# First MLP's single slots: Square, Tanh, h*e, h − tanh(h) and the copies of y at a higher scheduling priority

## The chip, the cores and the metric

The kernel runs on one core of a Trainium2 chip. The metric is the device time of one execution in microseconds (us). The engines that matter are TensorE (PE, matmuls; PEld is its weight load), VectorE (DVE), ScalarE (ACT), GpSimd (POOL) and SyncE (SP), which issues the DMAs. Each engine takes its instructions in the order in which they were laid down; one that waits for a semaphore holds up all that stand behind it on that engine.

## The reference

Four batches b, 8 heads, 576 tokens, 64 numbers per head; x is 2304 × 512 and both MLPs go 512 → 2048 → 512:

```
A  = softmax(q @ k_lm.T / 8)      # k_lm, q_lm: means of k, q over 18 tokens each, 32 landmarks
Bm = softmax(q_lm @ k_lm.T / 8);  C = softmax(q_lm @ k.T / 8)
Z  = Newton iteration for inverse(Bm), 6 times:  Z = 2 Z - Z Bm Z
x  = concat_heads(A @ Z @ C @ v)
h  = x @ w1_in;  x = (h - tanh(h)) @ w1_out                       # first MLP
h  = x @ w2_in;  out = (h * tanh(log(1 + exp(h)))) @ w2_out       # second MLP
```

## The kernel before, in words

The attention's last product is fused with the first MLP. P = (Z·C·v)·w1_in is formed for a pair of heads, A is transposed to AT, and h = P·AT comes out directly. P, AT, weights and the activations g are split into a high and a low part; three matmuls (hi·hi, lo·hi, hi·lo) replace one of full precision. From slot 16 on g is split as well.

**Slots.** The first MLP is cut into 128 slots. Slot s has batch b = s // 32, half batch hf = s // 16 % 2 (288 tokens) and feature block f = s % 16, so its h is a 128 × 288 tile. Slots below 24 and from 104 on (`WIDE = (24, 104)`) go in pairs through one PSUM tile `hw` of two banks (`vec`). Slots 24 to 103 go one by one (`vec_one`) through two single PSUM banks `h`, used in turn. The change touches `vec_one` and `y1`.

**One single slot s**, in the order of the program text:
- ACT splits the high part of gg of slot s − 2 (L115), and POOL or DVE its low part (L116).
- PE has written h(s) (L773, or L777 to L779 where AT is split). ACT takes Square into e (L852) and Tanh into t (L853).
- POOL makes the mask e ≥ FT (mk, L854). ACT takes Exp and Square of e into q (L856, L857).
- DVE does for slot s − 1: g = q·g (`small`, L800), then the pick where the mask is set (`pick`, L804).
- DVE does for slot s: g = h·e (L865) and t = h − tanh(h) (L867). L867 is the last reader of h(s): when it ends, the bank is free for h(s + 2).
- PE does y1 of an older slot (LAG = 4): y += w·gg (L882, L883, L886). Four PSUM banks y hold a half batch's four 128 × 288 sums over its 16 slots. At f = 15 four ACT copies (L891, two for each half of the feature blocks) take y to SBUF, an SP DMA writes it to DRAM (ys, L892), and the next half batch's y1 may then start in these banks.

**What sets the order.** A tile scheduler places the instructions of a slot with those of the background: the next batch's attention (landmark means L424 on DVE, L433 and L435 on ACT; the Newton products L377 with L614 on DVE; the transposes and normalisation of A and C L666 to L696; P in L736 and L738), the first MLP's weights (L303, L305), and from slot 102 on the second MLP's weights and y in (L914 and others). It orders by a priority that `tc.high_priority(n)` raises by n places; `yield` in a slot's generator lets another stream's instruction come next in program order. From slot 116 on (SWITCH) the order is that of the program text.

The tiles' names in the rows: es = e, qs = q, ta = t, tb and tc = g of two pairs of slots in turn, mk = mask, raw = the copy of y in SBUF, c = a row block of A or C, yv = Newton's Z.

Of the kernel before, what the change touches and what calls it, by code (L numbers as in the profile page):

```python
# [15 lines left out]
ACTF = mybir.ActivationFunctionType  # L16
ALU = mybir.AluOpType
# [12 lines left out]
def kernel(  # L30
# [68 lines left out]
    V = nc.vector  # L99
    A = nc.scalar  # L100
# [39 lines left out]
    def raw_f32():  # L140
        return f32(raw_p.tile([128, 512, 4], U16, tag="raw", name="raw").rearrange("p f t -> p (f t)"))
# [601 lines left out]
    hp, sv, yps = {}, {}, {}  # L743
# [42 lines left out]
    def low_half(s):  # L786
        gg = gg_tile(s, F32R)
        with tc.high_priority(20):
            split(sv[s], gg[:, 0], gg[:, 1], late())
        sv[s], sv[s + 1] = gg[:, :, 0], gg[:, :, 1]  # L790

    def low_one(s):
        gg = (ggs[s - 1] if s % 2 else gg_tile(s, F32R))[:, :, s % 2]
        with tc.high_priority(20):
            split(sv[s][0], gg[:, 0], gg[:, 1], late())
        sv[s] = gg

    def small(g, q):
        with tc.high_priority(40):
            V.tensor_tensor(out=g, in0=q, in1=g, op=ALU.mult)  # L800

    def pick(g, mk, t):
        with tc.high_priority(40):
            V.copy_predicated(out=g, mask=mk, data=t)  # L804
# [39 lines left out]
    def vec_one(s):  # L844
        i = s % 2
        if s == WIDE[0]:
            low_half(s - 2)
        elif s > WIDE[0] + 1:
            low_one(s - 2)
        h, e, q, mk = hp.pop(s), ES[:, i], QS[:, i], MK[-1][:, i]  # L850
        t, g = TA[:, i], (TB, TC)[s // 2 % 2][:, i]
        A.activation(out=e, in_=h, func=ACTF.Square)  # L852
        A.activation(out=t, in_=h, func=ACTF.Tanh)  # L853
        G.tensor_scalar(out=mk, in0=e, scalar1=FT, scalar2=None, op0=ALU.is_ge)  # L854
        with tc.high_priority(40):
            A.activation(out=q, in_=e, func=ACTF.Exp, scale=FK)  # L856
            A.activation(out=q, in_=q, func=ACTF.Square, scale=FB, bias=bias_c[:, 0:1])  # L857
        sv[s] = (g, t, q, mk)
        if s > WIDE[0]:
            g0, t0, q0, mk0 = sv[s - 1]  # L860
            small(g0, q0)
            yield 0
            pick(g0, mk0, t0)
            yield 0
        V.tensor_tensor(out=g, in0=h, in1=e, op=ALU.mult)  # L865
        yield 0
        V.tensor_tensor(out=t, in0=h, in1=t, op=ALU.subtract)  # L867
        yield 1

    def y1(s, half):  # L870
        f = s % 16
        gg = sv[s]
        w = W1o[f]
        for d in (2 * half, 2 * half + 1) if s < NW else ():
            if f == 0:
                yps[d] = ps_y.tile([128, 512], F32, tag="y", name="y")[:, 0:HS]
            mm(yps[d], w[:, 0, 128 * d:128 * d + 128], gg, start=(f == 0), stop=(f == NF - 1))
        for d in (2 * half, 2 * half + 1) if s >= NW else ():
            if f == 0:
                yps[d] = ps_y.tile([128, 512], F32, tag="y", name="y")[:, 0:HS]  # L880
            c = slice(128 * d, 128 * d + 128)
            mm(yps[d], w[:, 0, c], gg[:, 0, :], start=(f == 0), stop=False)  # L882
            mm(yps[d], w[:, 1, c], gg[:, 0, :], start=False, stop=False)  # L883
        for d in (2 * half, 2 * half + 1) if s >= NW else ():
            c = slice(128 * d, 128 * d + 128)
            mm(yps[d], w[:, 0, c], gg[:, 1, :], start=False, stop=(f == NF - 1))  # L886
        if f == NF - 1:
            o = (raw_f32() if s < NS - 1 else p2["yf"].tile([128, 2, C2], F32, tag="yf", name="yf").rearrange(
                "p a n -> p (a n)"))[:, 0:2 * HS].rearrange("p (d n) -> p d n", d=2)
            for d in range(2):  # L890
                A.activation(out=o[:, d], in_=yps[2 * half + d], func=ACTF.Copy)  # L891
            nc.sync.dma_start(out=ys[s // 16][:, 2 * half:2 * half + 2], in_=o)  # L892


# [162 lines left out]
    def pair(s, bg):  # L1057
        cur[0] = s
        v = vec(s) if wide(s) else None
        if s == WIDE[1]:  # L1060
            two_banks()
        if v:
            h1(s)
            h1(s + 1)
        for i in (s, s + 1):
            cur[0] = i
            if not v:
                h1(i)
            if i >= LAG:
                y1(i - LAG, 0)  # L1070
            mix, tail = bg(i)
            for g in mix + tail:
                part(g)
            if i >= LAG:
                y1(i - LAG, 1)
            parts([v or vec_one(i)] + mix)
            parts(tail)
# [4 lines left out]
    def group(k, bg2):  # L1082
        if k:
            units = o2_units(k - 1)
        for p in range(7):
            product(k, p)
            if k:
                for _ in range(UNITS[p]):
                    next(units)
            else:  # L1090
                for x in LAST[p]:
                    y1(NS - LAG + x // 2, x % 2)
                if p == 5:
                    ph1.close()
                    for name, bufs in (("g3", 3), ("yl", 2), ("st", 2)):
                        p2[name] = ctx.enter_context(tc.tile_pool(name=name, bufs=bufs))
            mix = bg2(k, p)
            for g in mix:
                part(g)
            parts([combine(k, p)] + mix)  # L1100
        if k:
            assert next(units, None) is None
# [240 lines left out]
```

## Time and profile before

| | |
|---|---|
| median of 3 runs | 824.63 us (822.94, 824.63, 828.34) |
| the profiled execution | 824.84 us; its span on the core 823.1 us |
| PE busy | 786.2 us, 96% of the span |
| DVE, ACT, POOL busy | 587.2, 494.9, 192.9 us (71%, 60%, 23%) |
| first MLP's single slots | about 116 to 364 us of the span |
| second MLP | about 446 us to the end |

The span is what the core's instructions cover; the execution's own time is 1.7 us longer. The page gives busy time by engine, the span in 40 slices, the chain of work that ended last, groups of instructions by line, and DMA issues. In the rows further down, "[0.75 <-DVE ta L867]" says that the engine sat idle for 0.75 us before this row and that the write of ta by DVE at line 867 released it. Consecutive rows of an engine overlap a little, since instructions are pipelined: the cost of one is better read from start to start.

### The profile page before, as it was taken

What the parts mean: (1) busy time and instruction counts of PE and PEld (TensorE: products, weight loads), DVE (VectorE), ACT (ScalarE), POOL (GpSimd) and SP (SyncE); (2) the same over time, 40 slices, a digit from 0 to 9 for tenths busy, and PEclk for the clock granted to TensorE, in tenths of its full rate; (3) what the DMA queues carried; (4) which work ended last, traced back from release to release, by engine and by line L of the source; (5) the groups of instructions that cost most, each with busy time, mean ns of one, the idle gap of its engine ahead of it and who ended that gap; (6) DMA issues with size and microseconds to landing.
All of it is one profiled execution on the core that took longest, in us unless ns stands there. A gap on an engine that the chain in (4) does not pass through costs nothing. (4 is left out here: it accounts for less than half of the span.)

```text
span 823.1 us, 14641 instructions
## 1 busy us (share of the span) xinstructions
PE 786.2 (96%) x5473; PEld 677.4 (82%) x5473; DVE 587.2 (71%) x1179; ACT 494.9 (60%) x1102; POOL 192.9 (23%) x215
## 2 busy tenths in 40 slices
PE   8889999999999999989998999999999999999996
PEld 4556787799978888779997888888888888889885
DVE  7799999898699977899987877885333356334332
ACT  5677877787678876785786566556223236223222
POOL 0000028765678656752220000000000000000000
PEclk9999999999999999999999999999999999999999
DMA  8898933414043001150327757864425424523402
GB/s 275 268 310 290 362 111 101 155 37 146 1 160 133 1 31 53 52 157 1 131 90 251 247 209 274 279 231 163 179 90 186 160 91 152 193 90 114 155 1 76
DMA packets 42022, 123.61 MB, mean 150 GB/s; under 512 B 5856, under 2 KB 14560, under 8 KB 38880
## 3 DMA queue, kind: packets, MB, share of 16 engines
q1 hardware_dynamic: 41952, 122.68, 42.5%
q8 instruction: 43, 0.70, 0.4%
q14 instruction: 27, 0.22, 0.1%
HBM read 94.36 MB, written 28.31 MB: 149 GB/s over the span
## 5 line engine op out<-in xcount | busy, mean ns | idle before, releaser
L983 ACT ACTIVATE gg<-x 128x384 fp32r<-128x384 f32 x72 | 37.8, 525 | 170.4 <-DVE x L993 170.4
L882 PE MATMUL y<-gg,w 128*128 128x288 f32 x448 | 132.8, 311 | 5.0 <-ACT raw L891 3.9
L883 PE MATMUL y<-gg,w 128*128 128x288 f32 x448 | 125.9, 295 | 0.0
L854 POOL TENSOR_SCALAR mk<-es 128x288 uint8<-128x288 f32 x80 | 78.5, 982 | 138.2 <-DVE yv L614 114.4
L882 PEld LDWEIGHTS y<-gg,w 128*128 128x128 f32 x448 | 84.1, 188 | 24.4 <-issue 15.2
L972 PE MATMUL h<-yk,P 128*128 128x384 f32 x288 | 97.6, 339 | 3.4 <-DVE P L208 3.4
L970 PE MATMUL h<-yk,P 128*128 128x384 f32 x288 | 97.5, 338 | 1.7 <-ACT yf L891 0.6
L971 PE MATMUL h<-yk,P 128*128 128x384 f32 x288 | 96.9, 336 | 0.0
L886 PE MATMUL y<-gg,w 128*128 128x288 f32 x448 | 96.0, 295 | 0.0
L986 DVE TENSOR_TENSOR gg<-x,gg 128x384 fp32r<-128x384 f32 x72 | 40.2, 558 | 68.4 <-ACT x L984 66.6
L883 PEld LDWEIGHTS y<-gg,w 128*128 128x128 f32 x448 | 84.3, 188 | 0.7 <-issue 0.2
L993 DVE TENSOR_TENSOR x<-x,h 128x384 f32<-128x384 f32 x72 | 39.8, 552 | 57.9 <-PE h L972 57.9
L1030 PE MATMUL y<-w,gg 128*128 128x512 f32 x192 | 76.3, 398 | 0.0
L1029 PE MATMUL y<-w,gg 128*128 128x512 f32 x192 | 76.2, 397 | 0.0
L1028 PE MATMUL y<-w,gg 128*128 128x512 f32 x192 | 75.8, 395 | 0.0
L886 PEld LDWEIGHTS y<-gg,w 128*128 128x128 f32 x448 | 71.8, 188 | 0.2
L970 PEld LDWEIGHTS h<-yk,P 128*128 128x128 f32 x288 | 54.3, 189 | 9.7 <-issue 1.4
L151 ACT ACTIVATE top<-raw 128x512 f16<-128x512 bf16 x64 | 49.9, 786 | 20.2 <-DVE X L185 6.1
L972 PEld LDWEIGHTS h<-yk,P 128*128 128x128 f32 x288 | 54.3, 189 | 5.9 <-DVE P L208 5.9
L971 PEld LDWEIGHTS h<-yk,P 128*128 128x128 f32 x288 | 54.2, 188 | 5.9
L116 POOL TENSOR_TENSOR gg<-tc,gg 128x288 fp32r<-128x288 f32 (+1 forms) x45 | 39.9, 894 | 39.6 <-ACT gg L115 36.0
L116 POOL TENSOR_TENSOR gg<-tb,gg 128x288 fp32r<-128x288 f32 (+1 forms) x44 | 40.4, 922 | 32.3 <-ACT gg L115 24.5
(214 smaller groups left out, 1947.2 us busy)
## 6 DMA issues: line engine op xcount, KB each, us to landing
P<-w2s SPq DMA_DIRECT2D x16, 1024.0 KB, 4.8
w<-w1s SPq DMA_DIRECT2D x24, 512.0 KB, 4.4
P<-w2s SPq DMA_DIRECT2D x16, 768.0 KB, 5.7
w2s<-P SPq DMA_DIRECT2D x8, 1024.0 KB, 3.9
raw<-in_w1i_dram SPq DMA_DIRECT2D x16, 511.8 KB, 5.1
raw<-in_w1o_dram SPq DMA_DIRECT2D x16, 511.8 KB, 5.1
raw<-in_w2i_dram SPq DMA_DIRECT2D x16, 511.8 KB, 4.2
raw<-in_w2o_dram SPq DMA_DIRECT2D x16, 511.8 KB, 4.5
```

The source lines that it names most:

```text
L116: eng.tensor_tensor(out=L, in0=src, in1=f32(H), op=ALU.subtract)
L151: A.activation(out=top[:, :, 1], in_=raw.bitcast(BF16)[:, :, 2], func=ACTF.Copy)
L854: G.tensor_scalar(out=mk, in0=e, scalar1=FT, scalar2=None, op0=ALU.is_ge)
L882: mm(yps[d], w[:, 0, c], gg[:, 0, :], start=(f == 0), stop=False)
L883: mm(yps[d], w[:, 1, c], gg[:, 0, :], start=False, stop=False)
L886: mm(yps[d], w[:, 0, c], gg[:, 1, :], start=False, stop=(f == NF - 1))
L970: mm(t, w[:, i, 0, c], y[a][:, 0], start=(a == 0), stop=False)
L971: mm(t, w[:, i, 0, c], y[a][:, 1], start=False, stop=False)
L972: mm(t, w[:, i, 1, c], y[a][:, 0], start=False, stop=(a == 1))
L1028: mm(q, gg[:, 0, cs], w[:, 0, :], start=first, stop=False)
L1029: mm(q, gg[:, 0, cs], w[:, 1, :], start=False, stop=False)
L1030: mm(q, gg[:, 1, cs], w[:, 0, :], start=False, stop=last)
```

## The change

Square and Tanh of a single slot, h·e and h − tanh(h), and the two copies per half of a y go into blocks `tc.high_priority(70)`; the `yield 0` between h·e and h − tanh(h) goes. No instruction is added or removed: each engine has the same ones in another order. `small`, `pick`, Exp and Square of e keep their 40, the splits their 20.

```diff
         t, g = TA[:, i], (TB, TC)[s // 2 % 2][:, i]
-        A.activation(out=e, in_=h, func=ACTF.Square)
-        A.activation(out=t, in_=h, func=ACTF.Tanh)
+        with tc.high_priority(70):
+            A.activation(out=e, in_=h, func=ACTF.Square)
+            A.activation(out=t, in_=h, func=ACTF.Tanh)
         G.tensor_scalar(out=mk, in0=e, scalar1=FT, scalar2=None, op0=ALU.is_ge)
...
-        V.tensor_tensor(out=g, in0=h, in1=e, op=ALU.mult)
-        yield 0
-        V.tensor_tensor(out=t, in0=h, in1=t, op=ALU.subtract)
+        with tc.high_priority(70):
+            V.tensor_tensor(out=g, in0=h, in1=e, op=ALU.mult)
+            V.tensor_tensor(out=t, in0=h, in1=t, op=ALU.subtract)
         yield 1
...
-            for d in range(2):
-                A.activation(out=o[:, d], in_=yps[2 * half + d], func=ACTF.Copy)
+            with tc.high_priority(70):
+                for d in range(2):
+                    A.activation(out=o[:, d], in_=yps[2 * half + d], func=ACTF.Copy)
             nc.sync.dma_start(out=ys[s // 16][:, 2 * half:2 * half + 2], in_=o)
```

The lines of the kernel after are one to two numbers higher: L852, 853, 856, 857, 865, 867, 891, 892 become L853, 854, 857, 858, 867, 868, 893, 894.

**Place A: ACT while the wide slots 18 and 19 run** (99 to 103 us), where the first half batch's last y copy falls. L817, L818, L828 and L829 are the wide form of a slot's Square, Tanh, Exp and Square; L115 splits gg of slots 16 and 17; L303 is weights. Before, and then after:

```order
L817 ACTIVATE es<-hw 128x576
L818 ACTIVATE tb<-hw 128x576
L828 ACTIVATE qs<-es 128x576
L115 ACTIVATE gg<-tc 128x576
L829 ACTIVATE qs<-qs,bias_c 128x576
L303 ACTIVATE w<-w 128x512
L891 ACTIVATE raw<-y 128x288
```

```order
L817 ACTIVATE es<-hw 128x576
L893 ACTIVATE raw<-y 128x288
L828 ACTIVATE qs<-es 128x576
L818 ACTIVATE tb<-hw 128x576
L829 ACTIVATE qs<-qs,bias_c 128x576
L115 ACTIVATE gg<-tc 128x576
L303 ACTIVATE w<-w 128x512
```

The copy went up five places, and the split of gg now stands behind the copy and behind the second exponential step. On SP the DMA of this copy (L892, now L894) now stands before both of the next batch's loads of k (L408); it stood between them.

**Place B: DVE in slots 29 to 31** (133 to 137 us). L682 and L684 belong to the normalisation of C, L696 transposes it, L738 is the low part of P, L424 a landmark mean of k. Before, and then after:

```order
L738 TENSOR_TENSOR P<-m,P 128x512
L684 RECIPROCAL xm<-xm 128x9
L424 TENSOR_REDUCE red<-k 128x64
L865 TENSOR_TENSOR tb<-h,es 128x288
L867 TENSOR_TENSOR ta<-h,ta 128x288
L800 TENSOR_TENSOR tb<-qs,tb 128x288
L696 STREAM_TRANSPOSE c<-c 128x288
```

```order
L696 STREAM_TRANSPOSE c<-c 128x288
L684 RECIPROCAL xm<-xm 128x9
L738 TENSOR_TENSOR P<-m,P 128x512
L867 TENSOR_TENSOR tb<-h,es 128x288
L868 TENSOR_TENSOR ta<-h,ta 128x288
L696 STREAM_TRANSPOSE c<-c 128x288
L800 TENSOR_TENSOR tb<-qs,tb 128x288
L424 TENSOR_REDUCE red<-k 128x64
```

The mean stood ahead of the pair that frees the bank of h and now stands behind it; one transpose came ahead of the pair in its place.

**Place C: ACT where half batch 1 is copied out** (slots 35 and 36, 151 to 156 us). L736 is the high part of P, L115 AT<-c the high part of AT. Before, and then after:

```order
L115 ACTIVATE gg<-tb 128x288
L852 ACTIVATE es<-h 128x288
L853 ACTIVATE ta<-h 128x288
L856 ACTIVATE qs<-es 128x288
L891 ACTIVATE raw<-y 128x288
L857 ACTIVATE qs<-qs,bias_c 128x288
L891 ACTIVATE raw<-y 128x288
L736 ACTIVATE P<-m 128x512 x2
L115 ACTIVATE AT<-c 128x288
L891 ACTIVATE raw<-y 128x288 x2
```

```order
L853 ACTIVATE es<-h 128x288
L854 ACTIVATE ta<-h 128x288
L857 ACTIVATE qs<-es 128x288
L893 ACTIVATE raw<-y 128x288 x2
L858 ACTIVATE qs<-qs,bias_c 128x288
L115 ACTIVATE gg<-tb 128x288
L736 ACTIVATE P<-m 128x512 x2
L115 ACTIVATE AT<-c 128x288
L893 ACTIVATE raw<-y 128x288 x2
```

Copies 1 and 2 came up beside each other, and the split of gg went down. Copies 3 and 4 still stand behind P and the AT split.

## Rows read from the trace of the kernel before

**Rows 1.** Windows by stage: length, busy us of each engine, clock, DMA share, GB/s.

```profile
core 0: us, PE busy (x) PEld busy (x) DVE busy (x) ACT busy (x) POOL busy (x), PEclk, DMA share, GB/s
24.00:130.00 106.00, 97.77 (x772) 69.88 (x765) 97.17 (x187) 81.54 (x162) 10.45 (x11) 1.00 0.73 255
130.00:227.00 97.00, 94.20 (x900) 82.36 (x898) 82.89 (x195) 74.56 (x209) 65.65 (x76) 1.00 0.28 93
```

**Rows 2.** PE's waits: line that waited, releaser, us in total, times, longest.

```profile
PE y L882 <- ACT raw L891: 3.9, 4, 1.8
...
PE h L777 <- DVE ta L867: 2.9, 4, 1.3
PE hw L777 <- DVE ta L867: 2.0, 1, 2.0
```

**Rows 3.** Timeline of PE, rows at which it waited: start, length, instruction, wait.

```profile
100.81 0.53 PE L377 MATMUL m<-yv 32*32 32x96 f32 x16 [0.55 <-DVE yv L614]
101.73 0.40 PE L882 MATMUL y<-gg,w 128*128 128x288 f32 x1 [0.39 <-ACT gg L115]
...
136.05 0.75 PE L773 MATMUL h<-AT,P 128*128 128x288 f32 x2 [0.75 <-DVE ta L867]
...
155.98 0.40 PE L882 MATMUL y<-gg,w 128*128 128x288 f32 x1 [1.56 <-ACT raw L891]
...
234.34 0.40 PE L777 MATMUL h<-AT,P 128*128 128x288 f32 x1 [1.25 <-DVE ta L867]
...
352.02 0.40 PE L882 MATMUL y<-gg,w 128*128 128x288 f32 x1 [1.76 <-ACT raw L891]
```

**Rows 4.** Timeline of DVE at places B and C.

```profile
133.98 1.29 DVE L424 TENSOR_REDUCE red<-k 128x64 f32<-128x1152 f32 x1
135.19 0.44 DVE L865 TENSOR_TENSOR tb<-h,es 128x288 f32<-128x288 f32 x1
...
152.75 0.44 DVE L680 TENSOR_REDUCE xm<-c 128x9 f32<-128x288 f32 x1
153.11 0.58 DVE L804 COPY_PREDICATED tc<-mk,ta 128x288 f32<-128x288 uint8 x1
...
154.32 0.45 DVE L800 TENSOR_TENSOR tc<-qs,tc 128x288 f32<-128x288 f32 x1
154.69 0.47 DVE L696 STREAM_TRANSPOSE c<-c 128x288 f32<-128x288 f32 x1
```

**Rows 5.** Timeline of ACT at place C.

```profile
153.44 1.10 ACT L736 ACTIVATE P<-m 128x512 fp32r<-128x512 f32 x2
155.19 0.44 ACT L115 ACTIVATE AT<-c 128x288 fp32r<-128x288 f32 x1 [0.64 <-DVE c L696]
155.54 0.69 ACT L891 ACTIVATE raw<-y 128x288 f32<-128x288 f32 x2
```

**Rows 6.** Timeline of ACT at place A.

```profile
99.34 0.65 ACT L817 ACTIVATE es<-hw 128x576 f32<-128x576 f32 x1
99.89 0.65 ACT L818 ACTIVATE tb<-hw 128x576 f32<-128x576 f32 x1
100.42 0.69 ACT L828 ACTIVATE qs<-es 128x576 f32<-128x576 f32 x1
101.00 0.68 ACT L115 ACTIVATE gg<-tc 128x576 fp32r<-128x576 f32 x1
101.57 0.78 ACT L829 ACTIVATE qs<-qs,bias_c 128x576 f32<-128x576 f32 x1
```

**Rows 7.** Timeline of SP's queue at place A: the load of k, the store of y.

```profile
98.86 0.39 SPq L408 DMA_DIRECT2D k<-in_kT_dram  x1
```

**Rows 8.** The source line L408, all its loads from issue to landing.

```profile
DMA to landing us min/median/max: 3.8/6.0/8.9
```

**Rows 9.** Source lines L867 and L800: shortest, median and longest ns, then the forms.

```profile
L867 DVE TENSOR_TENSOR ta<-h,ta x80: 438/446/451, 118.7 to 363.8; 128x288 f32<-128x288 f32 x80
...
L800 DVE TENSOR_TENSOR tb<-qs,tb x46: 416/460/1478, 47.6 to 419.5; 128x288 f32<-128x288 f32 x40, 128x576 f32<-128x576 f32 x6
```

## The prediction

> **What bounds the kernel now.** I read the windows by stage first [rows 1]. In 130 to 227 us PE is busy for 94.20 of 97 us at full granted clock, and over the whole span the page has it at 96%. So the kernel is bound by PE almost everywhere, and only PE's idle time can be won. DVE (82.89 of 97) is next. The early stage, 24 to 130 us, is different: PE 97.77 and DVE 97.17 of 106, so there DVE is nearly as full as PE, and what is put ahead of something on DVE or ACT can reach PE.
>
> Next I read PE's waits by releaser [rows 2]. The change can only shorten waits for the banks of h (released by L867) and of y (released by the copies L891). They are 3.9 us in four waits on copies, 2.9 + 2.0 us in five waits on L867, and one more of 0.75 us at 136.05 [rows 3]: 9.5 us together, 1.2% of the time. That is the ceiling. It is concentrated in few places, so I went through these one by one: what stands before the releaser on its engine, and whether the new order moves it. The timeline of PE has the places [rows 3].
>
> **The change part by part.** Nothing is added, so each term is a place where the order differs.
>
> *Place B, 136.05 us.* PE waits 0.75 us for L867. On DVE the mean L424 starts at 133.98 and the pair at 135.19 [rows 4]: the mean costs the pair 1.21 us. It now stands behind the pair, and one transpose L696 (some 0.4 us, its row at 154.69 lasts 0.47 [rows 4]) stands ahead instead. The pair gains 1.21 − 0.40 = 0.8 us, more than the wait. Term: −0.75 us (between 0, if the transpose waits for POOL, and −0.75).
>
> *Place C, 151 to 160 us.* PE waits 1.56 us at 155.98 for copies 3 and 4 [rows 3]. They stand behind the AT split, which itself waited 0.64 us for DVE's transpose L696 [rows 5]. The copies were raised, yet in the new order they are still behind that split. What changes is that on DVE the L696 now comes ahead of an L800 (154.32 to 154.69, 0.37) and of L680 (152.75 to 153.11, 0.36) [rows 4]: 0.73 us earlier. ACT itself is done with P by 153.44 + 1.10 = 154.54 [rows 5], so the split can start at most 0.65 us earlier; the copies follow it. A little later PE waits for L867: rows 2 leave 2.9 − 1.25 − 1.3 = 0.35 us for two small waits [rows 2, 3], of which I count one, 0.2, here; it goes if the mean of q that stands before it on DVE is not late. I take −0.7 us for the place (bounds 0, if POOL delays L696, and −1.76, both waits).
>
> *The same switch in slots 67 and 68.* Rows 2 leave 3.9 − 1.56 − 1.76 = 0.6 us for the two smaller waits on copies, and the other half of the 0.35 us for L867. I take −0.2 us (0 to −0.8).
>
> *234.34, 331 and 352.02 us.* The two long waits on L867 (1.25 us at 234.34 [rows 3], and the 1.3 us that is the longest of its row [rows 2]) and the 1.76 us for copies at 352.02 [rows 3] are half of the ceiling. There ACT, DVE and POOL order the instructions ahead of the releaser as before: at 234 and 331 an L738 of two products stands ahead of the pair still, and copies 3 and 4 at 352 are behind the AT split still. Term: 0 for 4.3 us of waits.
>
> *Slots 102 to 106.* PE waits 2.0 us for L867 at the first wide h after the single slots [rows 2]. An L804 (0.58 us at most, by the row at 153.11 [rows 4]) stood ahead of the pair there and now stands behind it, but PE also reaches the first wide h three y matmuls sooner (0.4 us), so nothing of its own is won there; the matmuls that it passes are still worth their time later. I take −0.4 us (0 to −0.8).
>
> *Place A, 99 to 105 us: a loss.* The split of gg (L115) starts at 101.00 and its first reader on PE at 101.73 [rows 3, 6]. With the copy and the second exponential step ahead, the order L817, copy, L828, L818, L829, L115 gives, start to start from the rows: 99.34 + 0.55 + 0.29 + 0.58 + 0.53 + 0.67 = 101.96 instead of 101.00: 0.96 us later [rows 6] (0.29 is my value for one copy: two together last 0.69 [rows 5]). PE fills 0.53 us of this with a third Newton product that the new order pulls ahead (one x16 lasts 0.53 [rows 3]), which leaves 0.4 us. On DVE the mean L424 moves from 116.8 us to just behind the mask of slots 20 and 21, ahead of the wide pair that frees hw; by its length of 1.29 us [rows 4] the pair and the low split come 1.2 us later, and against a PE that idles 8 us in this stage [rows 1] I take half of it as lost, 0.7 us. Together +1.1 us. The lower bound is 0 (both covered), the upper +4.1 (rival 2).
>
> Of the rest: Square and Tanh in the middle of a batch already stand first in a slot, and the position of h against y1 on PE is the same in slots 25 to 103, so I give it nothing; what covers it is that PE is 97% busy there.
>
> Sum: −0.75 − 0.7 − 0.2 − 0.4 + 1.1 = −0.95 us. After each of these places PE is the bound, so a shift carries through to the end. From the profiled execution's own 824.84 us: 823.9 us. The median of the runs lies 0.2 us below that execution, so **823.7 us**.
>
> **The rivals.**
>
> *1. All waits that it aims at vanish.* From 9.5 us, nothing lost early: 824.6 − 9.5 = 815.1, or some 816 if the smaller ones stay. Against it: the order at 234, 331 and 352 is unchanged, and 4.3 us hang there. Chance 0.07.
>
> *2. The load of k comes late and the early stage pays: slower.* On SP, the first load of the next batch's k is issued at 98.86 [rows 7]. It now stands behind the store of a copy that ends at about 100.3, so I expect issue at about 100.7. A load of k takes 3.8 to 8.9 us to land, 6.0 in the median [rows 8]: 104.5 to 109.6. The mean L424 now stands on DVE at about 106.9, ahead of the wide pair of slots 20 and 21, and ACT's L433, which reads it, stands ahead of the next pair's Square. A load that lands at 109.6 keeps DVE idle for 2.7 us with the bank of hw behind it. With 1.2 us of the mean itself and 0.4 of the split, the early loss is about 4.1 us, and the sum −2.05 + 4.1 = +2.05: 826.7 us. It decides from the point at which the loss exceeds the 2.05 us of gains: when k lands later than about 107.9. For it: DMA is 73% busy in this stage [rows 1]. Against: the median landing is 106.7. Chance 0.18.
>
> *3. The change does nothing to be measured.* The gains at places B and C are given back at the next wait on the same engines: 824.6 us. Since DVE has 14.1 us spare in 97 [rows 1], a delay needn't return. Chance 0.10.
>
> *4. DVE becomes the bound.* L867 reads one tile from SBUF and h from PSUM, and never stretches: 438 to 451 ns; L800 reads two from SBUF and goes from 416 to 1478 ns [rows 9]. With L865 and L867 side by side, L800 and L804 of neighbouring slots fall together more often, beside POOL's mask and split (65.65 of 97 us busy [rows 1]). DVE's spare time of 14.1 us in 32 slots is 0.44 us a slot. If the stretches grow past it, every further 0.1 us costs 8 us over 80 slots: 833 us and more. The Trainium skill, "SBUF — State Buffer", section "Who interferes with whom", states that a DVE instruction with two SBUF inputs contends with a GpSimd instruction that reads SBUF, whichever is second being held up whole, and that one with a single SBUF input does not; the trace agrees in L867's narrow and L800's wide spread, and by that rule the rival is a real mechanism. Against it: the set of such instructions is the same, and their number beside POOL hardly changes. Chance 0.06.
>
> **How the numbers follow.** My forecast has 0.59, the rivals 0.07, 0.18, 0.10 and 0.06. The forecast's own bounds: all gains at their largest (−0.75 − 1.76 − 0.8 − 0.8 = −4.1) and no loss give 820.5; gains at nothing and the loss at +1.1 give 825.7. The range reaches below to 819 for part of rival 1, and above past rival 2 to 828.5, the gains being 0 there (824.6 + 4.1 = 828.7). What stays out is rival 1 for the most part, rival 4 and the ends of 2: under 0.2. 1% is 8.2 us, about what a measurement of this kernel can tell from no change. Only the better half of rival 1 is faster by that (0.04), and only rival 4 slower (0.05); the rest, 0.91, is the same.
>
> **What would show it.** In the changed profile: no wait of h(31) on L868 at 135 us; at the switch near 155 us a wait on copies of about 0.9 us instead of 1.56; waits of 1.2 to 1.8 us still at 233, 330 and 351 us; y1's first matmul with split gg about 0.9 us later than 101.73. If the waits for copies are gone everywhere, the split was not what held them. If DVE has a wait for k's DMA before L424 near 107 us, rival 2 is at work. If L800 has a median well over 460 ns, it is rival 4. If PE's busy time itself changes by more than 1 us, I have missed something that is not a wait.

## The result: 830.2 us, 0.6% slower

The median of 16 runs of the changed kernel is 830.19 us (826.81 to 833.51). The kernel before, run beside it 16 times, has 824.96 us (822.21 to 828.34). The ratio is 1.0058, with a 95% interval of 1.0039 to 1.0077: a loss of 3.2 to 6.4 us, where 0.95 us of gain was forecast. It is under 1%, but on the wrong side, and outside the range.

### The profile after

The profiled execution took 827.00 us, its span 825.0. These are the windows by stage, which answer to [rows 1]:

```profile
core 0: us, PE busy (x) PEld busy (x) DVE busy (x) ACT busy (x) POOL busy (x), PEclk, DMA share, GB/s
24.00:130.00 106.00, 97.94 (x782) 70.00 (x778) 97.16 (x185) 79.42 (x157) 8.43 (x8) 1.00 0.73 256
130.00:227.00 97.00, 93.04 (x893) 81.80 (x879) 83.23 (x193) 74.19 (x207) 66.45 (x76) 1.00 0.28 94
```

PE is busy for 93.04 us between 130 and 227 us, where it was 94.20: 1.2 us more of waiting where most of the gain was expected. PE's waits by releaser, answering to [rows 2]:

```profile
PE h L777 <- DVE ta L868: 5.2, 4, 1.3
PE m L359 <- DVE P L738: 3.1, 3, 1.7
PE y L883 <- ACT raw L893: 2.6, 3, 2.1
```

Waits for the copies fell from 3.9 to 2.6 us, which looks like what was intended; but most of it is a late load in the trace of before (place C in the section on the prediction). Waits for the pair (h·e and h − tanh(h)) rose from 2.9 to 5.2 us, though the change raises the pair. A wait on L738, the low part of P, has become one of 1.7 us, in a line I did not list. The places are in PE's timeline, which answers to [rows 3]:

```profile
102.19 0.53 PE L377 MATMUL m<-yv 32*32 32x96 f32 x16 [0.47 <-DVE yv L614]
103.07 0.40 PE L883 MATMUL y<-gg,w 128*128 128x288 f32 x1 [0.35 <-ACT gg L115]
...
137.28 0.99 PE L773 MATMUL h<-AT,P 128*128 128x288 f32 x3 [0.68 <-DVE ta L868]
144.63 0.67 PE L359 MATMUL m<-q,kb 64*32 64x288 f32 x2 [1.72 <-DVE P L738]
157.12 0.40 PE L883 MATMUL y<-gg,w 128*128 128x288 f32 x1 [0.21 <-ACT raw L893]
161.95 0.41 PE L777 MATMUL h<-AT,P 128*128 128x288 f32 x1 [1.34 <-DVE ta L868]
...
236.54 0.40 PE L777 MATMUL h<-AT,P 128*128 128x288 f32 x1 [1.27 <-DVE ta L868]
259.99 0.40 PE L777 MATMUL h<-AT,P 128*128 128x288 f32 x1 [1.35 <-DVE ta L868]
355.13 0.40 PE L883 MATMUL y<-gg,w 128*128 128x288 f32 x1 [2.14 <-ACT raw L893]
367.88 0.37 PE L777 MATMUL hw<-AT,P 128*128 128x288 f32 x1 [1.38 <-DVE ta L868]
```

A wait costs time only if PE doesn't catch up, so I also took the start of each slot's first h matmul from the two traces, set their difference to zero at slot 16, and read where it grows. Where PE's own order of h and y1 differs, as in slots 20 to 26, a single slot's value is no cost; slots 27 and 28 have the same matmuls behind them in both:

| slot | 20 | 22 | 25 | 31 | 33 | 36 | 37 | 39 | 68 | 71 | 100 | 102 | 104 | 127 |
|---|---|---|---|---|---|---|---|---|---|---|---|---|---|---|
| after − before, us | +0.96 | +1.75 | −0.05 | +0.85 | +2.52 | +2.55 | +0.76 | +1.89 | +1.79 | +2.77 | +2.71 | +4.22 | +3.14 | +3.16 |

Place A costs 0.72 us by slot 28 and 0.85 by slot 31, place B another 1.67 by slot 33, place C seems to give 0.66 back, slots 68 to 71 cost 0.98, and 102 to 104 give back part of a step of 1.5 that is no wait but a stretch at a lower clock (below).

### The profile page after: what moved, and what is told of

Read it like the earlier page. It is cut to its first block, busy times and chain, and to the rows that moved or that the text cites. A ratio compares the mean times of both kernels' runs of the same rounds, so it can differ in the third digit from the quotient of the medians.

```text
span 825.0 us, 14649 instructions
## 1 busy us (share of the span) xinstructions
PE 785.5 (95%) x5472; PEld 677.1 (82%) x5473; DVE 589.2 (71%) x1179; ACT 494.7 (60%) x1102; POOL 193.3 (23%) x215
```

## Experiments

Times are medians, ratios are to the kernel before on the same chip. Slots are as in the table above, each from one execution: stretches at a lower clock are in them, and the trace of before holds 1.6 us of a late load between slots 36 and 39 (both below), so that −1.5 at slot 71 is no gain.

| kernel | median us | ratio [95%] | slot 31 | 33 | 71 | 127 |
|---|---|---|---|---|---|---|
| the change, second set of runs | 829.24 | 1.0060 [1.0034, 1.0085] | +1.64 | +4.50 | +6.18 | +6.86 |
| copies alone | 830.38 | 1.0071 [1.0053, 1.0088] | +3.45 | +4.87 | +5.38 | +6.06 |
| Square and Tanh alone | 828.04 | 1.0042 [1.0026, 1.0058] | +1.47 | +1.47 | +1.43 | +2.56 |
| the pair alone | 826.94 | 1.0023 [1.0011, 1.0036] | −0.12 | +1.25 | −0.35 | +1.34 |
| all but the copies | 828.55 | 1.0045 [1.0028, 1.0061] | +1.29 | +2.53 | +2.86 | +3.63 |
| change, shorter means | 825.06 | 0.9992 [0.9974, 1.0009] | +1.57 | +2.88 | +2.10 | +2.06 |
| change, AT split on DVE | 829.63 | 1.0045 [1.0025, 1.0064] | +0.68 | +3.55 | +2.98 | +3.38 |
| change, means in halves | 828.92 | 1.0046 [1.0024, 1.0068] | +0.32 | +3.67 | +3.32 | +4.09 |
| before, with filled waits | 826.36 | 1.0023 [1.0007, 1.0039] | 0.00 | −0.01 | −1.48 | −0.89 |

### Which part of the change costs

Each of these keeps only the named part of the diff shown above:

```diff
 copies_only  # L891's block only
 acts_only    # the block of Square and Tanh only
 pair_only    # the block of h·e and h − tanh(h) only
 no_copies    # both of these blocks, L891 as before
```

Copies alone. 

> Only the y copies at priority 70. Theory 1 (full stretches of DVE: what is taken from one wait comes back at the next): DVE's order at the switch of half batches 1 and 3 is that of the full change, with the split of gg behind the copies, so the wait for copies near 156 us falls from 1.56 to under 0.5 us and h then waits 1.0 to 1.4 us for h - tanh(h) near 161 and 259 us; place A loses 0.8 us as in the full change; 2 to 4 us over before. Theory 2 (the loss is place A's alone, and the copies are good after it): +0.8 us or less, no new wait at 161 or 259 us. Theory 3 (the loss comes from Square, Tanh and the pair): within 1 us of before.

All but the copies. 

> Square, Tanh and the pair at priority 70, the y copies as before. Theory 1: place A is as before (first y1 with split gg waits 0.4 us), the mean of q stands ahead of the pair as in the full change, so h waits over 0.5 us for the pair near 160 and 258 us, and the waits for copies (1.56 and 1.76 us) stay: 0 to 3 us over before. Theory 2: no loss, -1 to +0.5 us. Theory 3: the full +5 us.

The pair alone. 

> Only h*e and h - tanh(h) at 70, without the yield between them. Theory 1: early order unchanged; on DVE at the switches the mean of q goes ahead of an earlier pair, so the wait of 0.2 us near 159 us goes and another comes within 5 us of it: -1 to +2 us. Theory 2: no loss. Theory 3: up to +3 us.

Square and Tanh alone. 

> Only Square and Tanh at 70. Theory 1: DVE's order at the switches is that of the full change (one transpose ahead of the second pair, the mean of q ahead of the third), with the AT split ahead of half of P on ACT, so the copies' wait of 1.56 us falls by 0.5 us or more, and h waits near 160 us for the pair by about what is won: -1 to +2 us. Theory 2: no loss. Theory 3: up to +3 us.

Every part costs by itself, and the losses don't add up: 5.9, 3.5 and 1.9 us by the ratios, against 4.8 for the whole. With the copies alone 3.45 us are lost already at h(31), more than was expected of them, and the wait for the pair that was expected near 161 us isn't there. Nor did the wait for the copies fall below 0.5 us: it is 1.68 us at 161.53 (DVE waits 0.81 us for the load of q ahead of it) and 1.18 us at 259.48. DVE and PE of that kernel at place B:

```profile
137.19 0.48 DVE L696 STREAM_TRANSPOSE c<-c 128x288 f32<-128x288 f32 x1 [3.00 <-POOL c L686]
...
140.49 2.09 PE L773 MATMUL h<-AT,P 128*128 128x288 f32 x4 [3.18 <-DVE ta L867]
```

The raised copies do not stand here at all. They shifted the background's instructions by some places, and a transpose came to stand ahead of a pair while its input was still POOL's to finish: DVE idles 3.00 us, PE waits 3.18 us. With all but the copies, place A's loss is gone (−0.01 at slot 27): it belongs to the copies. But by slot 33 the same 2.53 us are lost, since 1.23 come in ahead of h(29), where PE's 16 products for the transposes (L359) come in two goes and the second is released by DVE's L666, and the waits for P's low part (1.28 us), and for the pair near 162 and 260 us (1.36 each), are there as in the change. At the end of half batch 1 that kernel has the same short wait for copies (0.26 us at 157.09) without raising them, so the copies' own priority won nothing there. With Square and Tanh alone the wait for the pair ahead of h(31) is 1.84 us (0.75 before), and the copies are waited for by 1.13 us near 157 and 1.14 us near 255 us. With the pair alone it is P's low part, 1.42 us at 142.62.

### Place B: what holds P's low part

Three kernels were to take the wait on L738 away. The first sums 2 of 18 tokens in the means L424. The second raises L800 and L804 of the slot before, so that they don't fall behind the raised pair. The third splits each mean of k and q in two.

```diff
 after_nomean
-  t[:, :, 0:S].rearrange("p a (m r) -> p a m r", r=R)
+  t[:, :, 0:S].rearrange("p a (m r) -> p a m r", r=R)[:, :, :, 0:2]
 after_pick (small and pick)
-        with tc.high_priority(40):
+        with tc.high_priority(110):
 after_half (the means, for every b)
-  V.tensor_reduce(out=red[:, g, x], ...)      # once
+  V.tensor_reduce(...)                        # for each half of t
```

Shorter means. 

> The full change, and the landmark means of batches 1 to 3 sum 2 of 18 tokens instead of all (part of the computation is left out), so that L424 lasts some 0.2 us instead of 1.3. Theory A (DVE is full around the switches, and the mean there is what a pair or a P waits behind): the waits of 1.34 us near 162 and 260 us and of 1.72 us for L738 near 144 us fall below 0.5 us each; 4 to 6 us under the full change. Theory B (VectorE held up beside GpSimd's splits is what makes the pair late): the wait near 162 us keeps 0.8 us or more; 1 to 2 us under. Theory C (the loss is the clock's alone, whatever waits): no more than 1 us under, unless the clock is higher.

Picks raised. 

> The full change, and small and pick (L800, L804) of the slot before at 110, so that they stand ahead of the raised pair. Theory D (the raised pair pushes pick back, so ACT's split of gg waits for it, and P's high part behind that split comes late, hence L738 and PE near 144 us): pick stands ahead of each pair between 138 and 144 us, the wait for L738 near 144 us falls from 1.7 to under 0.8 us; the wait of 1.3 us for the pair near 162 and 260 us stays; 1 to 2 us under the full change. Theory E (the means on DVE make L738 late, and there are two of them here in place of one): the wait near 144 us stays above 1.2 us; no gain.

Means in halves. 

> The full change, with each landmark mean of batches 1 to 3 in two instructions of half the length, so that a pair may stand between them. Theory A: the wait near 162 us falls by about half a mean, 0.6 us, and so does that near 260 us; the one for L738 near 144 us, which has both halves ahead of it, stays over 1 us; 1 to 2 us under the full change. Theory B: the waits near 162 and 260 us stay above 1 us; no gain. Theory C: no gain but by the clock.

None removed it. PE's timelines of the first, the second and the third:

```profile
143.24 1.31 PE L359 MATMUL m<-q,kb 64*32 64x288 f32 x16 [1.37 <-DVE P L738]
```

```profile
145.62 1.71 PE L359 MATMUL m<-q,kb 64*32 64x288 f32 x16 [1.86 <-DVE P L738]
```

```profile
145.43 1.80 PE L359 MATMUL m<-q,kb 64*32 64x288 f32 x16 [2.20 <-DVE P L735]
```

What the means do explain is the wait for the pair at 162 and 260 us: it is gone with short and with halved means, and a wait for the copies takes its place (1.48 us at 156.98 with short ones, 1.16 at 160.12 with halved ones). From h(36) to h(39) these two kernels take 10.13 and 9.79 us, where the change takes 10.49, so a part of the wait comes back as time. Shorter means bring the time back to that of before (0.9992), 4.2 us under the change as expected, but with the wait on L738 still there. They also leave out DVE work in every batch, so this is a bound and not a repair.

Raising the picks was tried without the change and with its pair alone too:

```diff
 before_pick, pair_pick (on before, and on pair_only)
-        with tc.high_priority(40):
+        with tc.high_priority(110):
 before_pick_atdve: this on before, and
-        split(at, ATt[b, hf][:, g, 0, :], ATt[b, hf][:, g, 1, :], E())
+        split(at, ATt[b, hf][:, g, 0, :], ATt[b, hf][:, g, 1, :], V if hf else E())
```

> The kernel before, with nothing but small and pick at 110. Its order at place A is that of before, at place B the mean of k stands behind the pair and the pick, at place C DVE has the full change's order but for pick ahead of the pair. Theory D: no wait of h at 136 us (0.75 before), none over 0.5 us near 142 us; copies at 156 us wait under 0.5 us (1.56 before), and the pair near 160 us waits 1.2 to 1.4 us, as VectorE stands beside three splits there; within 1 us of before, at the same clock. Theory E: over 1 us of wait for L738 near 142 us, 1 us over before.

> Only the pair at 70, as in pair_only, and small and pick at 110. Theory D: at place B pick is not behind a pair, so the 1.42 us for L738 that pair_only has near 142 us fall below 0.5 us; near 160 us the pair waits 1.2 to 1.4 us, as in the full change; 0 to 1 us under pair_only. Theory E: L738 is on time too, since no mean stands near it here (this run alone doesn't tell D from E).

> before_pick, and the low split of AT of each second half batch on VectorE. If GpSimd's three splits in a row are what holds VectorE up near 157 us, the pair's waits near 160 and 258 us are 0.6 us or less, where before_pick has 1.2 to 1.4, the copies' waits stay under 0.5 us, and the time is 1 to 2 us under before. If not: no better than before_pick.

The ratios are 1.0069 [1.0046, 1.0091], 1.0062 [1.0040, 1.0084] and 1.0073 [1.0047, 1.0098], and after_pick has 1.0066 [1.0045, 1.0087]: 5.1 to 6.0 us over, where at most 1 us over before was expected of the first and 1 to 2 us under before of the third. The wait on L738 appears without anything of the change (2.15 us at 145.75 in the kernel before with raised picks); with the pair and the picks raised the waits move to transposes (1.11 us for c L666 at 139.23) and to an AT split. So whichever part of a slot is raised, PE loses 1.2 to 3.9 us between slots 28 and 33 (stretches at a lower clock included), and what it waits for differs: the pair behind a transpose or a mean, P's low part, a transpose. That is what these runs share; which single instruction starts it stays open.

### Place C: POOL's split of AT given to DVE

```diff
 after_atdve (on the change)
-        split(at, ATt[b, hf][:, g, 0, :], ATt[b, hf][:, g, 1, :], E())
+        split(at, ATt[b, hf][:, g, 0, :], ATt[b, hf][:, g, 1, :], V if hf else E())
```

> The full change, with the low split of AT of each second half batch on VectorE instead of GpSimd (6 instructions, some 0.4 us each). Theory B: with one of three splits gone from GpSimd between 155 and 159 us, L800, L804 and L682 there last 0.5 us less each, and the wait for the pair near 162 us falls below 0.7 us; 1 to 2 us under the full change. Theory A: the wait grows by 0.3 us or stays; 0 to 1 us over. Theory C: no change beyond what the clock gives.

The wait for the pair at place C falls from 1.34 to 0.53 us, below the bound that was set. DVE and PE in that kernel:

```profile
160.23 0.47 DVE L804 COPY_PREDICATED tc<-mk,ta 128x288 f32<-128x288 uint8 x1
160.60 0.16 DVE L682 TENSOR_SCALAR xm<-xm 128x9 f32<-128x9 f32 x1
...
164.42 0.40 PE L777 MATMUL h<-AT,P 128*128 128x288 f32 x1 [0.53 <-DVE ta L868]
```

L804 and L682 took 1.04 and 0.78 us at this place in the change, beside POOL's split. From h(36) to h(39) and from h(68) to h(71) this kernel takes 0.75 and 0.81 us less than the change in its first profile. So the mechanism is shown at both places; the time of the whole is not shown to be better (1.0045 against 1.0060, overlapping), and the mean clock of these runs was 0.991.

### The change again, and the clock

> The full change once more, for its clock. Theory C's part that I hold true beside A: the runs differ only by stretches at 1.2 GHz that follow PE's long waits, so the profile has the waits of the first profile to 0.1 us between 137 and 368 us, and a run of over 830 us has two or more such stretches, each right after a wait of over 1.2 us; each costs 1.5 to 1.8 us. Against it: different waits from run to run, or stretches at 1.2 GHz with no wait ahead.

The second profile of the unchanged diff has two things that the first had not. The load of k is late, and PE's clock falls behind more of its waits, four times in place of one (near 37, 146, 371 and 453 us). DVE, PE and the windows of that execution:

```profile
108.22 1.35 DVE L424 TENSOR_REDUCE red<-k 128x64 f32<-128x1152 f32 x1 [0.95 <-DMA k<-in_kT_dram]
...
145.54 0.43 PE L359 MATMUL m<-q,kb 64*32 64x288 f32 x1 [1.71 <-DVE P L738]
...
358.58 0.40 PE L883 MATMUL y<-gg,w 128*128 128x288 f32 x1 [2.12 <-ACT raw L893]
370.56 0.37 PE L777 MATMUL hw<-AT,P 128*128 128x288 f32 x1 [2.08 <-DVE ta L868]
```

```profile
142.00:146.00 4.00, 2.29 (x16) 1.73 (x15) 3.52 (x8) 3.77 (x11) 3.41 (x5) 1.00 0.73 264
146.00:150.00 4.00, 4.00 (x27) 2.94 (x27) 3.24 (x9) 1.15 (x4) 1.61 (x3) 0.57 0.35 96
...
370.00:374.00 4.00, 3.44 (x17) 3.47 (x18) 4.00 (x9) 3.45 (x8) 1.26 (x1) 0.69 0.13 50
```

The clock column reads 0.57 of 2.4 GHz right behind the wait of 1.71 us, so mostly the lower level of 1.2 GHz, while PE is busy for all 4.00 us. By these numbers a stretch takes (1 − 0.57) × 4 = 1.7 us of full clock away. The change's first profile has one behind the 2.14 us wait at 355.13, the step at slot 102; the profile of before has one too:

```profile
354.00:358.00 4.00, 2.87 (x16) 2.86 (x17) 3.09 (x7) 3.84 (x12) 2.98 (x4) 0.79 0.67 204
358.00:362.00 4.00, 4.00 (x33) 2.52 (x33) 3.36 (x7) 2.69 (x7) 1.57 (x2) 0.78 0.85 241
```

```profile
446.00:450.00 4.00, 4.00 (x14) 3.41 (x13) 1.76 (x3) 1.78 (x3) 0.00 (x0) 0.58 0.99 344
```

Not every wait of this length has one, and the same wait has one in one execution and none in the next: 2.14 us at 355.13 brought one in the first profile, 2.12 us at 358.58 none in the second. The waits themselves agree between the two profiles to 0.1 us from 137 to 361 us, as expected, but for one of 0.40 us that only the second has (at 181.20); the one ahead of the first wide h does not (1.38 and 2.08 us, explained in the next section). Over the runs, (1 − mean clock) × span is 7.15 us in the mean of the change's 16 runs and 6.29 in the 10 of its second set, against 4.94 in 31 runs of the kernel before. Not all of this sum is lost time: in the change's first profile the clock reads 0.82 from 818 to 822 us, where PE is busy for 0.17 us, and in the 16 traces here without raised attention the part behind PE's last matmul is 0.7 to 2.2 us of the sum. In the 16 runs the standard deviation of the span falls from 2.38 to 1.07 us when each run's own loss is subtracted; in the runs of the kernel before it hardly falls (1.72 to 1.51 in 31 runs) or grows (1.06 to 1.57 in 17), so the clock doesn't explain their spread.

To see whether waits cause it, matmuls of zeros into a finished y bank were put into four long waits of each kernel:

```diff
 before_fill; after_fill with {(58,1): 8, (90,1): 8, (96,0): 15, (99,1): 9}
+    FILL = {(58, 1): 8, (90, 1): 8, (96, 0): 12, (99, 1): 13}
 ...
+        for _ in range(FILL.get((s, half), 0)):
+            z = tops[0][:, :, 0]
+            mm(yps[2 * half], z[:, 0:128], z[:, 0:HS], start=False, stop=False)
```

> The kernel before, with matmuls by zeros (some 0.12 us each, added to a y bank, so that the sums stay) laid into PE's waits ahead of h at 234 and 331 us (8 each), of y at 352 us (12) and of the first wide h at 364 us (13). If the stretches at 1.2 GHz follow from PE standing still in such waits, the profile has none between 228 and 420 us, the mean clock of the runs rises from 0.994 to 0.995 or more, and the time is 0 to 2 us under before. If the clock falls for another reason, it is 0.994 still, and the time is that of before or up to 1 us more.

> The full change, with the same matmuls by zeros ahead of the same four places (8, 8, 15 and 9). If the waits bring the clock down, the profile has no stretch at 1.2 GHz between 228 and 420 us (each of the two profiles of the full change has one there, after 355 or after 367 us), the mean clock rises from 0.992 to 0.994 or more and the time is 1 to 2 us under the full change. If not: clock and time as in the full change.

The profile of the first has no stretch below full clock and took 822.61 us; that of the second has none from 228 to 420 us. The mean clocks rose (.9940 to .9952, and from between .9914 and .9924 to .9933). But the times did not fall: 1.0023 [1.0007, 1.0039], and 1.0092 [1.0061, 1.0122]. So the expectation on the time failed. Nor does the first profile say much, as the profile of before has no stretch between 228 and 420 us either. In the runs of the filled kernel before the loss by the clock is 1.0 us lower (3.92 against 4.94), but the span less that loss is 2.9 us longer (820.7 against 817.8); where that comes from is open, and that a shorter wait would bring the 1.7 us back is not shown.

### Raising the background too

If the background is what comes late, it should help to raise it with the slots:

```diff
 after_att (after_att2: p_gen(...) in hi(..., 70) as well; before_att: 30, on before)
-                    gens["a"] = attn_all(b + 1)
+                    gens["a"] = hi(attn_all(b + 1), 70)
-                    gens["al"] = both(attn_a, b, 1)
+                    gens["al"] = hi(both(attn_a, b, 1), 70) if b else both(attn_a, b, 1)
```

> The full change, and the next batch's attention (means, normalisation, transposes and the AT splits of batches 1 to 3) at 70 as well. Theory F (what the raised slot work costs is that it pushes the attention's steps into the switch of batches and half batches, where P's low part and the pair then come late): the transposes, the means and the AT splits stand earlier, no wait over 0.6 us for L738 near 144 us and none over 0.6 us for the pair near 162 and 260 us; 2 to 5 us under the full change. Against it: waits of over 1 us near 144 and 162 us as in the full change, or as long ones elsewhere before 170 us, and no gain.

> As after_att, and the products and splits that make P at 70 too. Theory F: P's low part goes up on VectorE in addition, no wait for it at all near 144 us; at most 1 us under after_att. Against it: as for after_att.

> The kernel before, with only the next batch's attention at 30. Theory F: the AT split comes earlier, so the copies' waits near 156 and 253 us (0.4 us when the load of q is on time, 1.6 when it is late) go, and the wait of 0.75 us at 136 us with them; 0 to 2 us under before. Against it: the raised attention pushes the slots' own work back and h waits for its bank instead; 0 to 3 us over.

The ratios are 1.158 [1.1551, 1.1609], 1.1404 [1.1375, 1.1434] and 1.1361 [1.1315, 1.1406], so all three expectations failed. PE's waits between 130 and 180 us didn't go either: the longest are 2.66 us for L738 at 149.79, 2.69 us for the copies at 165.75 and 2.91 us for the pair at 137.26. By the signs that were set this speaks against theory F; but most of the time goes another way (last section), so whether a smaller raise would help stays open.

## Why the prediction was wrong

The step that failed is the pricing of places B and C and of slots 67 to 71: what the new order puts ahead of the pair and of P was counted with the lengths of one old trace, and a wait of that trace was taken for the order's. Forecast −0.75, −0.7 and −0.2 us, they measured +1.67, +0.94 and +0.98. The loss by the clock, which no term has, rose by 1.4 to 2.2 us in the mean of the runs.

**Place A: right in size, one term of two.** Forecast +1.1, measured +0.72 by slot 28 and +0.85 by slot 31. The first y1 matmul with split gg starts at 103.07 instead of 101.73; its place began 0.38 us later already (L817 at 99.72, before 99.34), so 0.96 us are its own, where 0.9 were forecast. PE's third Newton product stands ahead of it as worked out, and waits 0.47 us itself. From h(16) to h(28) PE idles 0.43 us more than before, where 0.4 were forecast for the split. The 0.7 us for the mean did not come as a wait: in this execution PE doesn't wait for hw behind it. It does in the second profile, 0.65 us at 110.95, with the load of k late. So the total came near for a reason that was only half right.

**Place B: the step that failed first.** I took the 0.75 us wait for the pair at h(31) as gone, by counting what stands ahead of the pair on DVE with its lengths in the old trace. Of the L682 there, before and then in the change:

```profile
133.19 0.16 DVE L682 TENSOR_SCALAR xm<-xm 128x9 f32<-128x9 f32 x1
```

```profile
132.31 0.64 DVE L682 TENSOR_SCALAR xm<-xm 128x9 f32<-128x9 f32 x1
133.44 0.45 DVE L680 TENSOR_REDUCE xm<-c 128x9 f32<-128x288 f32 x1 [0.48 <-ACT c L674]
...
134.25 0.64 DVE L682 TENSOR_SCALAR xm<-xm 128x9 f32<-128x9 f32 x1
...
137.88 1.34 DVE L424 TENSOR_REDUCE red<-k 128x64 f32<-128x1152 f32 x1
...
143.89 1.28 DVE L738 TENSOR_TENSOR P<-m,P 128x512 fp32r<-128x512 f32 x2
```

The mean did move behind the pair. But a second round of the normalisation (L680, L682) came ahead of the pair with the transpose; the lists of place B begin behind it. Both L682, on a 128 × 9 tile, now run beside a tensor_tensor of POOL and last 0.64 us each, where before the one at 133.19 lasted 0.16, and DVE waits 0.48 us for ACT between them. The wait stays at 0.68 us. Then comes what I had not looked at: who is behind the mean. ACT's timeline has it:

```profile
137.65 0.44 ACT L115 ACTIVATE AT<-c 128x288 fp32r<-128x288 f32 x1 [0.55 <-DVE c L696]
...
140.58 0.45 ACT L115 ACTIVATE gg<-tb 128x288 fp32r<-128x288 f32 x1 [0.84 <-DVE tb L804]
...
142.43 1.07 ACT L736 ACTIVATE P<-m 128x512 fp32r<-128x512 f32 x2
```

A split of gg waits 0.84 us for an L804 that stands behind the mean and the next pair; P's high part stands behind that split (142.43, against 139.38 before), its low part behind the high one, and PE waits 1.72 us for it. The forecast −0.75 became +1.67. The shorter mean left 1.37 us of that wait, and with the picks (L804) raised it was 1.86, so neither the mean nor that L804 is the cause by itself; which instruction is stays open.

**Place C: the term rested on a late load, and a cost was left out.** The 1.56 us that PE waited for copies [rows 3] are not the order's. In the trace of before DVE idles for the load of q some 6 us ahead of the place; in the kernel with filled waits, which has the order of before up to there, it doesn't, and PE's wait is 0.43 us (the wait at the same switch one batch later is 0.41 us in the trace of before, at 253.14):

```profile
149.39 1.35 DVE L424 TENSOR_REDUCE red<-q 128x64 f32<-128x1152 f32 x1 [1.33 <-DMA q<-in_qT_dram]
```

```profile
147.47 1.34 DVE L424 TENSOR_REDUCE red<-q 128x64 f32<-128x1152 f32 x1
...
153.35 0.15 DVE L682 TENSOR_SCALAR xm<-xm 128x9 f32<-128x9 f32 x1
...
153.91 0.40 PE L883 MATMUL y<-gg,w 128*128 128x288 f32 x1 [0.43 <-ACT raw L895]
```

From h(36) to h(39) that kernel takes 9.56 us, before 11.15, the change 10.49. Against an execution whose load is in time the place costs 0.94 us instead of giving 0.66. The gain on the copies is real (0.43 to 0.21 us; 0.26 without raising them), but the pair is late by 1.34 us. DVE and POOL of the change, ahead of 161.95:

```profile
155.64 1.01 DVE L800 TENSOR_TENSOR tc<-qs,tc 128x288 f32<-128x288 f32 x1
...
156.95 1.04 DVE L804 COPY_PREDICATED tc<-mk,ta 128x288 f32<-128x288 uint8 x1
157.88 0.78 DVE L682 TENSOR_SCALAR xm<-xm 128x9 f32<-128x9 f32 x1
158.57 1.27 DVE L738 TENSOR_TENSOR P<-m,P 128x512 fp32r<-128x512 f32 x2
...
159.88 1.29 DVE L424 TENSOR_REDUCE red<-q 128x64 f32<-128x1152 f32 x1
```

```profile
155.53 0.81 POOL L116 TENSOR_TENSOR gg<-tb,gg 128x288 fp32r<-128x288 f32 x1 [0.33 <-ACT gg L115]
156.84 0.80 POOL L116 TENSOR_TENSOR AT<-c,AT 128x288 fp32r<-128x288 f32 x1 [0.49 <-ACT AT L115]
157.77 0.84 POOL L116 TENSOR_TENSOR gg<-tc,gg 128x288 fp32r<-128x288 f32 x1
```

Three POOL splits fall on three DVE instructions, each of which takes 0.5 to 0.6 us longer than elsewhere (L800 0.46 and L804 0.49 in the median, L682 0.16 at 160.60 above): 1.7 us, ahead of P, a mean and the pair. In the filled kernel, with the order of before, the same three took 0.70, 0.45 and 0.15 us at this place, 1.5 us less. This is rival 4's mechanism, at two places instead of in every slot; DVE is not the bound over a batch (83.23 of 97 us). By the Trainium skill, "SBUF — State Buffer", section "Who interferes with whom", tensor_scalar is among the instructions that can take the port pair shared with GpSimd. The trace agrees: L682, with one small SBUF input, goes from 0.16 to 0.78 us. The prediction had from that section that one SBUF input does not contend, without this exception, and gave such instructions no cost. Over its 16 instructions L682 takes 0.12 to 0.39 us where no tensor_tensor of POOL is running when it starts and 0.63 to 0.78 where one is, and its median goes from 0.23 to 0.63 us with the change.

**Slots 67 to 71: the same failure.** Forecast −0.2, measured +0.98: the wait for the pair at 259.99 is 1.35 us. Here before had no late load (9.54 us from h(68) to h(71), now 10.52), so this place shows the cost of place C without the filled kernel.

**The waits at 234, 331 and 352: right.** 1.27 us at 236.54 for 1.25; 2.14 at 355.13 for 1.76 is somewhat more, as in the other kernels with raised copies and the AT split as before (2.12 to 2.15), but it costs nothing: from h(100) to h(102) the second profile takes 8.40 us, before 8.43.

**Slots 102 to 106: right.** PE reaches the first wide h three y matmuls sooner, as worked out: 0.35 us less from h(102) to h(104) in the second profile. The wait falls from 2.03 to 1.38 us in the first profile, and slots 100 to 127 gain 1.05 us net of the clock's 1.5, where 0.4 was forecast. But the shorter wait is not the change's: in the second profile it is 2.08 us. In the 14 traces here with neither filled waits nor raised attention, it is 1.30 to 1.38 us in the seven whose clock fell behind the wait for the copies near 352 us, and 2.03 to 2.08 us in the other seven, whatever their order; a PE that was slowed comes later and finds less to wait for. Without these 0.65 us the gain is the 0.4 us of the forecast.

**Rival 2** is real in part of the executions: DVE's wait for k is 0.16 us in the first profile, 0.95 in the second, with h(31) at +1.64 there. It was no rival to the forecast but a term with a spread. (The early loss in its text, 2.7 + 1.2 + 0.4, is 4.3 us and not 4.1.)

**The clock: not among my terms.** The places sum to 0.85 + 1.67 + 0.94 + 0.98 − 0.40 = 4.0 us, almost all of it waits: PE's busy time is 785.5 us, before 786.2. The mean loss by the clock rose by 1.4 (second set) to 2.2 us (16 runs). Together that is 5.4 to 6.2 us, more than the 4.8 measured (0.58% of 824.96). That is no surprise: a stretch costs less than its loss where it shortens a later wait, as in slot 104, and the places are those of one execution. The runs by themselves give the lower end: the mean span less each run's own loss is 820.7 us in the 16 runs and 821.2 in the second set, against 818.6 in 31 runs of the kernel before, so 2.1 to 2.7 us that the clock does not explain. By these two counts the new order costs 2 to 4 us by itself, and the clock likely the rest; closer than that the runs don't show. That the clock's part comes from the new waits is likely by its place behind them, but the filled kernels did not confirm it.

So the profiled execution of before was no typical one, though its time is that of the median: it held 1.6 us of a late load, part of which I counted as something to win, and a loss by the clock of 0.003 × 823 = 2.5 us, 2.4 under the mean: one stretch near 446 us, and 0.8 us behind PE's last matmul.

## What to carry to other kernels

Raising the priority of a slot's work in a schedule shared with background work can move any background instruction by some places, also far from what was raised: before costing what comes earlier, list what PE reads next from the background (P, AT, transposes) and look who now stands ahead of its producers on each engine. Before a wait is counted as winnable, follow it back past its releaser, to a DMA if need be, and find the same place in another half batch (here 260 us): what is missing there belongs to that execution and not to the order. Where an instruction is moved beside GpSimd work, cost it by its longest row and not by its median.

## What the runs showed of the hardware that was not expected

A kernel whose PE is 95% busy still loses time to the clock: 4.94 us in the mean of 31 runs, or an estimated 2.7 to 4.2 us without the 0.7 to 2.2 us that the traces have behind PE's last matmul. The stretches at the lower of the two levels in the profile of before and the two of the change (near 446; 356; 37, 146, 371 and 453 us) each stood behind a wait of PE of 1.6 to 2.1 us; whether a given wait brings one differs between executions.

A tiny DVE instruction can cost as much as a large one: the tensor_scalar on 128 × 9 (L682) took 0.78 us beside a POOL split of 128 × 288, and 0.16 us without it.

Small matmuls laid between large ones cost far more here than in a row. With the attention raised, the 128 × 32 products came in twos between the 128 × 128 ones. PE in the kernel before with raised attention, the window, and then the products in a row as before:

```profile
344.87 0.42 PE L591 MATMUL m<-v,k 128*32 128x64 f32 x2
345.22 0.61 PE L777 MATMUL h<-AT,P 128*128 128x288 f32 x1
345.75 0.42 PE L591 MATMUL m<-v,k 128*32 128x64 f32 x2
```

```profile
344.00:348.00 4.00, 4.00 (x16) 2.15 (x15) 0.00 (x0) 0.30 (x1) 0.15 (x1) 0.50 0.00 0
```

```profile
96.76 0.89 PE L591 MATMUL m<-v,k 128*32 128x64 f32 x39
```

Two small products and one large one take 0.88 us from start to start, at a granted clock of 0.50, though PE is shown busy for all of the 4 us; 39 small ones in a row take 0.89 us, at full granted clock. The three kernels with raised attention lost 112 to 130 us by the ratios, and (1 − mean clock) × span is 68 to 79 us in them, against 4.9 in the kernel before beside them, so more than half of the loss stands with the clock. What makes the clock stay low while PE is shown busy is not shown; these rows show the pattern, and I did not count how much of the loss it makes up.
